# Direct instead of seven-product second matmuls in the first three expert groups of an attention and expert-mixing kernel, with batch 0's chunks in the freed PSUM banks

## The chip, the cores and the metric

The kernel runs on one NeuronCore of one Trainium2 chip, in one launch. The metric is the device time of one execution in microseconds (us). Before the change the median of 9 runs is 932.55 us, with a lowest of 931.42 and a highest of 934.4.

## The reference

Two blocks run one after the other, all in float32. The first is linear attention over batch 4, heads 4, sequence 1088, head size 32, with a feature map that is the outer product of two 8-wide projections. The second is a mixture of 8 experts over the 4352 tokens that the first block leaves, with a Sinkhorn-normalised weight for each token and expert.

```python
phi(x) = outer(S1 x, S2 x)                        # 8 x 8 = 64 features
kv, z  = sum_s phi(k)_s v_s,  sum_s phi(k)_s
attn   = (phi(q) kv) / (phi(q) z + 1e-6)
x      = attn as (4352, 128)
P      = exp(x w_gate - max);  8 rounds of row and column normalisation
out    = sum over e of  P[:, e] * (relu(x w1[e]) w2[e])   # w1: 128x1024, w2: 1024x128
```

## The kernel before

**Where the work is.** Nearly all TensorE work is the two expert products. The first product, `relu(x w1[e])`, is written by `first` (L916), and ScalarE's Relu (L920) moves it from a PSUM bank to the tile `hb` or `hx`. The second product, with `w2[e]`, is written by `into` (L1089). Both are cut into matmuls with 64 output columns. `tile_position` puts each in the left or the right half of the array, so two of them run side by side; I call them half 0 and half 1.

**Fewer products.** A plain block product of the second kind would need eight half matmuls for each block of two hidden slices and two token tiles. `seven` uses a Winograd form with seven. It needs sums and differences of the Relu outputs (`two.sums`, three VectorE instructions a block, L933), sums of the weights (`sums_of_two`, four GpSimd instructions per expert, L203 to L206), and a recombination when a group of tokens is done (`part_of_seven`: seven ScalarE copies at L751 to L766 and six VectorE additions at L742 and L745). `four` and `twenty` do the same with larger blocks in the later part.

**Groups.** `groups` lists token ranges with the experts that are applied to them. The first eight are unweighted: they need no routing weight `P`, so they can run while attention and routing are still going on. Their results go to `kept` and are weighted later. Groups 0 to 2 are 2 x 256 tokens with expert 0, 2 x 288 with expert 0, and 2 x 256 with expert 1, all in batch 0's tokens. Groups 3 to 6 (416 and 384 wide) follow with expert 0, group 7 with expert 1. From `PLAIN` on the groups are weighted and need `P`.

**Order by hand.** The order on VectorE and TensorE is that of the program text (`manual_schedule`). `steps` is a generator that yields after each quarter or eighth of a block. `fill(n)` draws steps from it until their `share` sums to n. Around it the main program lays the steps of the attention: for batch 0 in chunks (`query_products` L382 and L388, `multiply` L397, `fractions` L405, `divide` L416 to L423), and for batches 1 to 3 `keys_ab` (L317, L322), `keys_products` (L334), `keys_sums` (L350), `keys_kept` (L366, L368), `times` (L466), `tops` (L475, L479), `over` (L488 to L494), `transpose_q` (L300), `queries_ab` (L439, L442). Then comes `routing`: the logits (L509), the maximum (L598) and eight rounds (L609 to L625, with TensorE at L619).

**A path through DRAM.** For batches 1 to 3 the projected queries go out to DRAM and come back repeated over partitions: `queries_ab` writes `qa` and `qb` (L446, L450), `repeat_a` reads `ph` (L456) and `repeat_b` reads `rb` (L459). `times` multiplies the two. SyncE's queue (SP) issues most of these transfers, with the loads of `kx`, `qx`, `v` and the weights between them.

**PSUM.** There are eight banks. Four, tag `a`, are shared by everything through `bank()`. Four, tags `s0` to `s3`, hold the sums of a group's second product; `query_products` uses them once for chunk 0.

Of the kernel before, what the change touches and what calls it, by code (L numbers as in the profile page):

```python
# [10 lines left out]
F32 = mybir.dt.float32  # L11
# [39 lines left out]
def kernel(  # L51
# [12 lines left out]
    nc = tc.nc  # L64
# [304 lines left out]

    chunks = ((0, 512), (512, 800), (800, S))  # L370

    def query_products(c, i):


        lo, hi = chunks[c]
        n = hi - lo
        if c == 0:
            banks = [[mps.tile([P, 512], F32, tag=f"s{2 * i + m}", name="s") for m in range(2)] for i in range(2)]
            for m in range(2):
                for i in range(2):  # L380
                    sl = slice(64 * i, 64 * (i + 1))
                    nc.tensor.matmul(banks[i][m][:, 0:n], wqf[sl, m, :], qT[sl, lo:hi], start=True, stop=True,  # L382
                                     tile_position=(64 * i, 0))
        else:
            banks = {i: [bank(), bank()]}
            for m in range(2):
                for s in range(2):
                    nc.tensor.matmul(banks[i][m][64 * s:64 * (s + 1), 0:n],  # L388
                                     wz[:, m, 2 * i + s].rearrange("p i j -> p (i j)"), qT[:, lo:hi],
                                     start=True, stop=True, tile_position=(0, 64 * s))  # L390
        for j in range(2) if c == 0 else (i,):
            nc.scalar.copy(phs[0][:, j, lo:hi], banks[j][0][:, 0:n])
            queries[0, c, j] = banks[j][1][:, 0:n]
# [5 lines left out]
    def fractions(c, m):  # L399

        lo, hi = chunks[c]
        n = hi - lo
        t = queries[0, c, "pn", m] = bank()
        for i in range(2):
            nc.tensor.matmul(t[64 * i:64 * (i + 1), 0:n], kvz[:, m, i].rearrange("p h d -> p (h d)"),  # L405
                             phs[0][:, i, lo:hi], start=True, stop=True, tile_position=(0, 64 * i))
# [177 lines left out]
    def routing():  # L584
# [45 lines left out]
        for b in (1, 0, 2, 3):  # L630
# [15 lines left out]
              *((1088 + 832 * i, 416, 2, [0], False) for i in range(3)), (3584, 384, 2, [0], False),  # L646
              (512, 384, 2, [1], False)]
    PLAIN = len(groups)
    for lo in (1280, 512, 2048, 2816, 3584):
        groups.append((lo, NT3, 3, list(range(2 if lo == 512 else 1, E)), True))  # L650
    groups.append((0, 256, 2, list(range(2, E)), True))
# [3 lines left out]
    items = [(g, e) for g, group in enumerate(groups) for e in group[3]]  # L655
    loaded_w, sources, sums, parts, done = {}, {}, {}, {}, {}
    soon, later = [], []

    def tiles_of(j):
        return groups[items[j][0]][2]  # L660
# [62 lines left out]

    def part(g, k):

        if groups[g][2] == 3:
            part_of_twenty(g, k)
        elif g < len(groups) - 1:
            part_of_seven(g, k)
        else:  # L730
            last_part(g, k)
# [190 lines left out]
    def two(k):  # L922

        j, q = blocks[k]
        n = groups[items[j][0]][1]
        h, ts, (later_h, earlier_h, t13) = hs[k] = room_of(k)

        def step(c):
            f, t = 2 * q + c // 2, c % 2
            first(k, f, t * n, (t + 1) * n, h[c], k % 2)  # L930

        def less(out, a, b):
            nc.vector.tensor_tensor(out, a, b, op=Alu.subtract)  # L933

        def sums(c):

            if k == len(blocks) - 1:
                if c == 4:
                    less(ts[0], h[1], h[0])
                    less(ts[2], h[3], ts[0])  # L940
                    less(ts[1], h[3], h[1])
                    less(ts[3], h[2], ts[2])
            elif c == 4:
                less(t13, later_h, earlier_h)
            elif c == 5:
                less(ts[2], h[3], ts[0])
                less(ts[3], h[2], ts[2])

        return 4, step, sums
# [4 lines left out]
    def four(k):  # L954
        j, q = blocks[k]
        h = hs[k] = room_of(k)
        pqg = hs["pqg"]
        order = ((0, 0), (3, 0), (3, 1), (0, 1), (1, 0), (2, 0), (1, 1), (2, 1))

        def at(f, t):  # L960
            return 4 * t + f

        def step(c):
            f, last = order[c]
            if last:
                first(k, 4 * q + f, 2 * NT3, 3 * NT3, h[:, at(f, 2)], False)
            else:
                first(k, 4 * q + f, 0, 2 * NT3, h[:, f:f + 8:4], False)

        def places(*bs):  # L970
            if len(bs) == 1:
                return h[:, bs[0]]
            if bs[0] == bs[1]:
                return h[:, bs[0]:bs[0] + 1].to_broadcast([P, 2, NT3])
            return h[:, bs[0]:bs[1] + 1:bs[1] - bs[0]]

        def do(out, a, b, off=False):
            nc.vector.tensor_tensor(out if not isinstance(out, tuple) else places(*out), places(*a),  # L978
                                    places(*b) if isinstance(b, tuple) else b, op=Alu.subtract if off else Alu.add)

        def sums(c):
            if c == 2:
                do((U4, U2), (at(0, 0), at(3, 0)), (at(0, 1), at(3, 1)))
            elif c == 3:
                do((U1,), (at(3, 0),), (at(3, 2),))
            elif c == 4:
                do((V4,), (U1,), (at(0, 2),))
            elif c == 6:
                do((V3, V1), (U4, U2), (at(1, 1), at(2, 1)), True)
                do(pqg[:, 0:2], (at(1, 1), at(3, 1)), (at(0, 1), at(2, 1)), True)  # L990
            elif c == 7:
                do((W1, W2), (V4, V4), pqg[:, 0:2])
                do(pqg[:, 2], (V3,), (at(1, 0),), True)
            elif c == 8:
                do((U3, BB), (at(2, 0), at(1, 2)), (at(2, 2), at(2, 2)))
            elif c == 9:
                do((V2, W3), (U3, BB), (at(1, 2), V1))
                nc.vector.tensor_tensor(h[:, W4], pqg[:, 2], h[:, V2], op=Alu.subtract)

        return 8, step, sums  # L1000

    def weighted_of(k):
        return groups[items[blocks[k][0]][0]][4]
# [69 lines left out]
    def into(g, w, x, i, s, place):  # L1073

        lo, n, t, es, _ = groups[g]
        if g not in sums:
            sums[g] = [mps.tile([P, 512], F32, tag=f"s{i}", name="s")[:, 0:n * (t - 1)] for i in range(4)]
            done[g] = {}


        last = g == len(groups) - 1
        seen = done[g]
        c = seen[i, s] = seen.get((i, s), 0) + 1
        per = len(es) * (FO // (4 if t == 3 else 2)) * TIMES[t][i][s]
        if t == 2 and i == 3:
            per //= 2
        if last and (i, s) in ((1, 0), (1, 1), (2, 0), (3, 1)):
            per += 1
        nc.tensor.matmul(sums[g][i][H2 * s:H2 * (s + 1), n * place:n * (place + 1)], w, x, start=c == 1,  # L1089
                         stop=c == per, tile_position=(0, H2 * s))  # L1090
        if c == per:
            seen[i] = seen.get(i, 0) + 1
            if seen[i] == 2:
                part(g, i)
# [4 lines left out]
    def steps():  # L1099

        todo, sums_at, t = {}, {}, 0
        for k in range(len(blocks) + 5):
# [5 lines left out]
            if k < len(blocks):  # L1108
# [3 lines left out]
                if q == 0:  # L1112
                    for i in (j, j + 1, j + 2 if 0 < j and j + 2 < first_weighted else j):
                        if i < len(items) and i not in sources and (pools or i < first_weighted):
                            prepare_x(i)
                        if i < len(items) and i not in loaded_w and (pools or i < first_weighted):
                            prepare_w(i)
                if q == 1 and not weighted and loaded_w.get(j + 1, (0,))[-1] is None:
                    w1, w2, _ = loaded_w[j + 1]
                    loaded_w[j + 1] = w1, w2, sums_of_two(items[j + 1][1], w2)  # L1120
                if q == 0:
                    if weighted and e == es[3 if tiles == 3 else 2]:
                        weigh_kept(g)
                if k == len(blocks) - HELD:
                    kept_to_sums(g)
                m, step, sums_ = (four if tiles == 3 else two)(k)
                products = (twenty if tiles == 3 else seven)
            for c in range(m if k < len(blocks) else 4):
                if k < len(blocks):
                    step(c)  # L1130
# [6 lines left out]
                if k < len(blocks) and c == 0:  # L1137
                    for i in range(2, 10):
                        sums_at.setdefault(t + i, []).append(lambda i=i, f=sums_: f(i))
                    if k < len(blocks) - 2:  # L1140
                        for i, ps in enumerate(products(k)):
                            todo.setdefault(t + LAG + i, []).extend((k, p) for p in ps)
                share = n / 480
                if k >= len(blocks):
                    while later:
                        later.pop(0)()
# [19 lines left out]
    with tc.manual_schedule(engines={engines.DVE, engines.PE, engines.Activation}):  # L1166
# [14 lines left out]
        transpose_q(0, chunks[0][1])  # L1181
        fractions(0, 1)
        queries_ab(1)
        first_w = *first_w[0:2], sums_of_two(0, first_w[1])
        fractions(0, 0)
        query_products(1, 0)
        repeat_a(1)
        repeat_b(1)
        divide(0)
        load_q(2)  # L1190
    with tc.manual_schedule(engines={engines.DVE, engines.PE}):
        fill(0.6)
        multiply(1, 0)
        query_products(1, 1)
        fill(0.6)
        multiply(1, 1)
        transpose_k(1)
        load_k(2)
        fill(0.6)
        fractions(1, 1)  # L1200
        fractions(1, 0)
        keys_ab(1)
        fill(0.6)
        divide(1)
        keys_products(1, 0)
        fill(0.6)
        query_products(2, 0)
        fill(0.6)
        multiply(2, 0)
        query_products(2, 1)  # L1210
        keys_products(1, 1)
        fill(0.6)
        multiply(2, 1)
        fill(0.6)
        fractions(2, 1)
        fractions(2, 0)
        fill(0.6)
        divide(2)
        load_v(2)
        load_q(3)  # L1220
        keys_products(1, 2)
        fill(0.75)
        for b in range(1, B):
            for n in attention(b):
                fill(n)
# [38 lines left out]
```

## Time and profile before

| | before |
|---|---|
| median of 9 runs | 932.55 us (931.42 to 934.4) |
| profiled execution, its own time | 933.92 us |
| its span | 932.1 us |
| mean granted TensorE clock | 0.996 |
| TensorE busy | 919.1 us (99%), 7448 records |
| VectorE busy | 698.0 us (75%) |
| ScalarE busy | 417.5 us (45%) |
| GpSimd busy | 210.5 us (23%) |

A busy line counts the time in which at least one instruction of an engine is under way. Each float32 matmul of the program leaves two records on TensorE, so a pair of matmuls, one in each half, shows as x4. In the profile's names `a` is a tile in the shared banks, `s` one in the sum banks; the arrow points from what is read to what is written. "L916" is a line of the kernel. In a view of waits, "A <- B" means that A stood idle until B was done.

### The profile page before, as it was taken

How to read it: one execution, taken by the hardware profiler on the slowest of the kernel's cores; microseconds unless marked ns; L12 is line 12 of the kernel's file. 1: busy time of each engine (PE TensorE's matmuls, PEld its weight loads, DVE VectorE, ACT ScalarE, POOL GpSimd, SP SyncE). 2: the span in 40 equal slices, each digit the busy share in tenths (PEclk: the TensorE clock that was granted, in tenths of full speed). 3: DMA queues.
4: the chain of work that ended last, by engine and by line, in shares of the span. 5: the costliest groups of instructions: out<-in, count | busy, mean ns of one | idle time of the engine just before them, and what ended most of it. 6: DMA issues, size and time to landing. Idle time of an engine off the chain costs nothing.

```text
span 932.1 us, 18913 instructions
## 1 busy us (share of the span) xinstructions
PE 919.1 (99%) x7448; PEld 576.9 (62%) x7448; DVE 698.0 (75%) x1196; ACT 417.5 (45%) x903; POOL 210.5 (23%) x219
## 2 busy tenths in 40 slices
PE   8989999999999999999999999999999999999997
PEld 6667644567777777765555555555555555556875
DVE  6878689989778888586886656975757977668565
ACT  3345354564444454434544444544445444445443
POOL 4021100056655502130020101201110333210220
PEclk9999999999999999999999999999999999999999
DMA  9886100133345535354353534354434456452640
GB/s 254 262 249 216 53 1 1 30 102 108 108 142 166 181 112 164 108 184 134 120 152 124 176 108 147 111 179 135 137 118 146 151 157 192 158 182 90 173 152 12
DMA packets 91305, 128.15 MB, mean 137 GB/s; under 512 B 25392, under 2 KB 69504, under 8 KB 86480
## 3 DMA queue, kind: packets, MB, share of 16 engines
q1 hardware_dynamic: 88384, 121.42, 41.6%
q0 software_dynamic: 1600, 5.36, 2.0%
q8 instruction: 58, 0.95, 0.4%
q10 hardware_dynamic: 1232, 0.16, 0.1%
q14 instruction: 31, 0.25, 0.1%
HBM read 107.88 MB, written 19.05 MB: 136 GB/s over the span
## 4 chain that ended last, share of the span: by engine, by line
PE 93%; DVE 5%; issue 1%; ACT 1%; POOL 0%; DVEq 0%; ACTq 0%; POOLq 0%
PE a L916 48%; PE s L1089 40%; DVE hb L933 1%; PE a L350 1%; PE a L475 1%; PE a L114 1%; DVE hb L978 1%; PE a L439 0%; PE a L317 0%; ACT hb L920 0%; PE a L509 0%; DVE kp L334 0%; DVE pqg L978 0%; DVE cs L615 0%; PE a L388 0%
## 5 line engine op out<-in xcount | busy, mean ns | idle before, releaser
L916 PE MATMUL a<-xe,w 128*64 128x256 f32 (+1 forms) x2560 | 523.4, 470 | 0.0
L920 ACT ACTIVATE hb<-a 128x256 f32<-128x256 f32 (+4 forms) x408 | 194.8, 479 | 256.9 <-PE a L916 228.8
L920 ACT ACTIVATE hx<-a 128x256 f32<-128x256 f32 (+1 forms) x360 | 167.1, 464 | 214.3 <-PE a L916 195.5
L916 PEld LDWEIGHTS a<-xe,w 128*64 128x64 f32 x2560 | 215.6, 137 | 70.4
L1089 PE MATMUL s<-hb,ws 128*64 128x256 f32 (+3 forms) x1344 | 240.7, 395 | 0.6 <-DVE hb L978 0.6
L1089 PE MATMUL s<-hx,ws 128*64 128x256 f32 x1280 | 207.5, 379 | 0.0
L978 DVE TENSOR_TENSOR hx<-hx 128x512 f32<-128x512 f32 (+1 forms) x204 | 155.0, 770 | 67.7 <-ACT hx L920 62.8
L978 DVE TENSOR_TENSOR hb<-hb 128x512 f32<-128x512 f32 (+1 forms) x204 | 134.9, 672 | 90.7 <-ACT hb L920 86.6
L685 POOL TENSOR_TENSOR xe<-xT,xe 128x768 f32<-128x768 f32 (+2 forms) x41 | 84.9, 2071 | 506.4 <-DMA xe<-pT 385.3
L1089 PEld LDWEIGHTS s<-hb,ws 128*64 128x64 f32 x1344 | 117.3, 137 | 104.7 <-issue 76.5
L1089 PEld LDWEIGHTS s<-hx,ws 128*64 128x64 f32 x1280 | 110.4, 137 | 92.2 <-issue 71.1
L916 PE MATMUL a<-xT,w 128*64 128x416 f32 (+3 forms) x512 | 121.1, 466 | 0.8 <-ACT ab L320 0.6
L1089 PE MATMUL s<-hb,w 128*64 128x256 f32 (+3 forms) x496 | 102.1, 411 | 0.5 <-DVE kept L745 0.5
L933 DVE TENSOR_TENSOR hb<-hb 128x416 f32<-128x416 f32 (+7 forms) x96 | 65.5, 684 | 24.3 <-ACT hb L920 14.6
L1089 PE MATMUL s<-hx,w 128*64 128x256 f32 x384 | 68.9, 379 | 0.0
L916 PEld LDWEIGHTS a<-xT,w 128*64 128x64 f32 x512 | 50.8, 138 | 27.2 <-issue 13.0
L242 POOL TENSOR_TENSOR ws<-w 128x256 f32<-128x256 f32 (+1 forms) x70 | 60.9, 904 | 7.5 <-DMA w<-in_moe_w_dram 4.1
L1089 PEld LDWEIGHTS s<-hb,w 128*64 128x64 f32 x496 | 46.7, 137 | 23.9 <-issue 7.6
L933 DVE TENSOR_TENSOR hx<-hx 128x256 f32<-128x256 f32 (+1 forms) x65 | 38.4, 596 | 25.2 <-ACT hx L920 22.7
L978 DVE TENSOR_TENSOR pqg<-hb 128x512 f32<-128x512 f32 x68 | 45.8, 714 | 0.0
L1089 PEld LDWEIGHTS s<-hx,w 128*64 128x64 f32 x384 | 35.1, 137 | 10.6
L978 DVE TENSOR_TENSOR pqg<-hx 128x512 f32<-128x512 f32 x68 | 36.3, 574 | 0.0
(177 smaller groups left out, 489.9 us busy)
## 6 DMA issues: line engine op xcount, KB each, us to landing
w<-in_moe_w_dram SPq DMA_DIRECT2D x82, 512.0 KB, 5.5
ws<-ws SPq DMA_DIRECT2D x34, 1024.0 KB, 4.9
xe<-pT SPq DMA_DIRECT2D x34, 384.0 KB, 3.9
ws<-ws SPq DMA_DIRECT2D x12, 512.0 KB, 4.6
ph<-qa SPq DMA_DIRECT2D x12, 288.0 KB, 5.8
rb<-qb SPq DMA_DIRECT2D x3, 1152.0 KB, 8.2
pb<-pT SPq DMA_DIRECT2D x6, 384.0 KB, 7.2
kx<-in_k_dram SPq DMA_DIRECT2D x4, 544.0 KB, 4.7
```

Source lines behind the costliest of these rows:

```text
L114: nc.tensor.matmul(warm[:, 0:P], ones, ones, start=True, stop=True)
L242: tc.keep_in_program_order(nc.gpsimd.tensor_tensor(ws[:, c:c + len(ns)], blocks(x), blocks(y), op=Alu.subtract if off else Alu.add))
L350: nc.tensor.matmul(pv[64 * s:64 * (s + 1), i], kp[0:n, H * t + h].rearrange("p i j -> p (i j)"), vx[0:n, slots[h], t, :], start=(t == 0 an ...
L475: nc.tensor.matmul(pn[64 * s:64 * (s + 1), t, 2 * i:2 * i + 2].rearrange("p h d -> p (h d)"), ph[:, i, s, 64 * t:64 * (t + 1)], kvs[b % 2] ...
L685: tc.keep_in_program_order(nc.gpsimd.tensor_tensor(out, x, pb, op=Alu.mult))
L916: nc.tensor.matmul(ph[sl], loaded_w[j][0][:, P * f + H2 * s:P * f + H2 * (s + 1)], sources[j][:, lo:hi], start=True, stop=True, tile_posit ...
L920: nc.scalar.activation(out=out, in_=ph, func=Act.Relu)
L933: nc.vector.tensor_tensor(out, a, b, op=Alu.subtract)
L978: nc.vector.tensor_tensor(out if not isinstance(out, tuple) else places(*out), places(*a), places(*b) if isinstance(b, tuple) else b, op=A ...
L1089: nc.tensor.matmul(sums[g][i][H2 * s:H2 * (s + 1), n * place:n * (place + 1)], w, x, start=c == 1, stop=c == per, tile_position=(0, H2 * s))
```

## The change

The first three groups (`DIRECT`) compute the second product block by block: for each Relu output, two half matmuls with the raw weights, eight per block, accumulated in two banks. Their VectorE sums and recombinations are left out, and `part` copies each finished bank to `kept` on ScalarE. Group 0 uses `s0` and `s1`, group 1 `s2` and `s3`, group 2 `s0` and `s1`. The banks `s2` and `s3` also take batch 0's `query_products(1, 0)` and the `fractions` of chunks 1 and 2. The weight sums of expert 0 are made later, ahead of group 3; those of expert 1 ahead of group 7; expert 1's weights are loaded earlier. The list of steps in which batch 0's chunks 1 and 2 are mixed with `fill` is written anew.

```diff
-    def query_products(c, i):
+    def query_products(c, i, sums=False):
...
-            banks = {i: [bank(), bank()]}
+            banks = {i: [mps.tile([P, 512], F32, tag=f"s{m + 2}", name="s") if sums else bank() for m in range(2)]}
...
-        t = queries[0, c, "pn", m] = bank()
+        t = queries[0, c, "pn", m] = mps.tile([P, 512], F32, tag=f"s{m + 2}", name="s") if c else bank()
...
+    DIRECT = (0, 1, 2)
...
+    def direct_of(j):
+        return items[j][0] in DIRECT
...
     def part(g, k):
-        if groups[g][2] == 3:
+        if g in DIRECT:
+            lo, n, _, es, _ = groups[g]
+            nc.scalar.copy(kept[es[0]][:, lo + k * n:lo + (k + 1) * n], sums[g][k])
+        elif groups[g][2] == 3:
...
         def sums(c):
+            if direct_of(j):
+                return
...
+    def eight(k):
+        j, q = blocks[k]
+        w2, h = loaded_w[j][1], hs[k][0]
+        return [[(w2[:, 2 * q + c // 2, H2 * s:H2 * (s + 1)], h[c], c % 2, s, 0) for s in range(2)] for c in range(4)]
...
-            sums[g] = [mps.tile([P, 512], F32, tag=f"s{i}", name="s")[:, 0:n * (t - 1)] for i in range(4)]
+            banks = range(2 * g, 2 * g + 2) if g in DIRECT else range(4)
+            sums[g] = [mps.tile([P, 512], F32, tag=f"s{i % 4}", name="s")[:, 0:n * (t - 1)] for i in banks]
...
-        if t == 2 and i == 3:
+        if g in DIRECT:
+            per = FO
+        elif t == 2 and i == 3:
...
+                if j == 0 and q == 2:
+                    prepare_w(2)
-                if q == 1 and not weighted and loaded_w.get(j + 1, (0,))[-1] is None:
+                if q == 1 and j + 1 < first_weighted and not direct_of(j + 1) and loaded_w[j + 1][2] is None:
                     w1, w2, _ = loaded_w[j + 1]
-                    loaded_w[j + 1] = w1, w2, sums_of_two(items[j + 1][1], w2)
+                    w = w1, w2, sums_of_two(items[j + 1][1], w2)
+                    loaded_w.update({i: w for i in loaded_w if items[i][1] == items[j + 1][1]})
...
-                products = (twenty if tiles == 3 else seven)
+                products = twenty if tiles == 3 else eight if g in DIRECT else seven
...
-                share = n / 480
+                share = n / 480 * (16 / 15 if g in DIRECT else 1)
...
-        first_w = *first_w[0:2], sums_of_two(0, first_w[1])
         fractions(0, 0)
-        query_products(1, 0)
+        query_products(1, 0, True)
+        query_products(1, 1)
...
-        fill(0.6)
-        multiply(1, 0)
-        query_products(1, 1)
-        fill(0.6)
-        multiply(1, 1)
+        for i in range(2):
+            multiply(1, i)
         transpose_k(1)
         load_k(2)
-        fill(0.6)
+        fill(0.75)
         fractions(1, 1)
         fractions(1, 0)
+        fill(0.75)
+        divide(1)
         keys_ab(1)
-        fill(0.6)
-        divide(1)
+        fill(0.75)
+        query_products(2, 0)
         keys_products(1, 0)
-        fill(0.6)
-        query_products(2, 0)
-        fill(0.6)
+        fill(0.75)
+        query_products(2, 1)
         multiply(2, 0)
-        query_products(2, 1)
         keys_products(1, 1)
-        fill(0.6)
+        fill(0.75)
         multiply(2, 1)
-        fill(0.6)
+        fill(0.75)
         fractions(2, 1)
         fractions(2, 0)
-        fill(0.6)
+        keys_products(1, 2)
+        fill(0.75)
         divide(2)
         load_v(2)
         load_q(3)
-        keys_products(1, 2)
-        fill(0.75)
+        fill(0.5)
```

## The prediction

> **What bounds it.** I read the page first, then windows by stage, TensorE's waits, and timelines of VectorE and SyncE where TensorE waits.
>
> ```profile
> PE 919.1 (99%) x7448; PEld 576.9 (62%) x7448; DVE 698.0 (75%) x1196; ACT 417.5 (45%) x903; POOL 210.5 (23%) x219
> ...
> PE 93%; DVE 5%; issue 1%; ACT 1%; POOL 0%; DVEq 0%; ACTq 0%; POOLq 0%
> ```
>
> TensorE bounds the kernel; only its idle time and its count of matmuls can move the end. The windows (length, then PE, PEld, DVE, ACT, POOL busy, clock, DMA share, GB/s) say where it idles:
>
> ```profile
> 20.00:34.00 14.00, 12.27 (x124) 6.92 (x122) 10.52 (x24) 5.19 (x14) 0.86 (x2) 1.00 0.92 300
> 40.00:55.00 15.00, 15.00 (x196) 12.00 (x192) 13.26 (x25) 8.70 (x23) 5.01 (x8) 1.00 0.87 278
> 55.00:62.00 7.00, 4.51 (x28) 3.29 (x28) 6.54 (x10) 0.82 (x2) 2.21 (x4) 0.76 1.05 346
> 198.00:932.00 734.00, 727.74 (x5652) 456.21 (x5648) 539.08 (x904) 327.25 (x698) 179.90 (x142) 1.00 0.44 139
> ```
>
> Idle time and the only dip of the clock lie before 62 us, and there VectorE is nearly full. TensorE's waits from 20 to 60 us name it:
>
> ```profile
> PE a L439 <- DVE qT L300: 2.5, 1, 2.5
> PE a L405 <- DVE ph L397: 0.9, 2, 0.7
> PE a L916 <- ACT ab L320: 0.6, 1, 0.6
> ```
>
> Here is VectorE's queue ahead of the longest of them (start, length, work):
>
> ```profile
> 52.14 0.43 DVE L745 TENSOR_TENSOR w<-s,r 64x256 f32<-64x256 f32 x1
> 52.60 2.38 DVE L933 TENSOR_TENSOR hb<-hb 128x288 f32<-128x288 f32 x2
> 54.90 0.42 DVE L742 TENSOR_TENSOR z<-z,w 128x256 f32<-128x256 f32 x1
> 55.23 1.22 DVE L334 TENSOR_TENSOR kp<-ab 128x1024 f32<-128x1024 f32 x1
> 56.37 1.30 DVE L300 STREAM_TRANSPOSE qT<-qx 128x1088 f32<-128x1088 f32 x1
> ```
>
> The first three rows are seven-product work, and the change removes them. In the second, one of two instructions took 1.89 us instead of 0.46 while GpSimd made weight sums.
>
> **A ledger of lost time.** I priced every matmul at its steady rate (a pair of half matmuls: 0.43 us at 256 columns, 0.48 at 288, 0.70 at 416, from successive starts in the timeline; 0.11 at 64, from L350's 36 matmuls whose starts span 2.0 us), summed in program order, and subtracted the sum from the trace's start times. Lost time is 3.1 us at batch 1's key projections (start 20.9), 6.7 at its key sums (33.7), 7.1 at its first `tops` (37.9), 10.6 at `queries_ab(3)` (57.8), 13.2 at batch 2's `tops` (70.4), 15.7 at the logits (113.8) and 19.5 at the last routing matmul (180.7). After that it stays between 19.0 and 19.8 to the end. So at most some 16 us can be won, all of it early.
>
> **Part by part: TensorE.** 96 second-product matmuls replace 84. Twelve more half matmuls, eight at 256 and four at 288, are 4 x 0.43 + 2 x 0.48 = 2.7 us, fully on the path.
>
> **VectorE.** Twelve blocks lose three instructions each (0.68 + 2 x 0.42 at 256; 0.76 + 2 x 0.46 at 288, the stretched one aside): 8 x 1.52 + 4 x 1.68 = 18.9 us. Three groups lose six additions of 0.38 to 0.46: 7.5 us. With the stretch this takes 27 to 28 us out of a queue that held TensorE up from 24 to 60 us. ScalarE swaps 21 copies (0.36 to 0.40) for 6 of 0.37 to 0.40; it is busy at most 60% there, so zero.
>
> **GpSimd, SyncE.** Expert 0's four sums (3.0 us) move behind `queries_ab(3)`'s transfers, expert 1's behind `take_over(3)`'s first ones. VectorE, stretched meanwhile, has slack at both places (it idles over 6 us at 112 to 118); if that cover went, one instruction would cost 1.4 us. Expert 1's weights (1 MB) pass ahead of `v` of batch 2 and `qx` of batch 3 on SyncE. They led batch 2's `qa` before as well, so the bytes ahead of that path are the same: zero, up to 2 us if the queue's order hurts.
>
> **Walking the new order.** I follow VectorE and TensorE with the rows' durations. `multiply(1, 1)` (0.45) ends near 18.7, the key transposes (1.24 + 0.20) at 20.1, key projections start at 20.6 (lost: 2.8). `divide(1)` takes 2.0, then products 1.22, multiply 0.45, products 1.22, multiply 0.45, products 0.41, all without block sums between: done at 26.1. TensorE reaches the key sums at 28.5, with 25.6 of work done (27.1 before): lost 2.95 instead of 6.7. They and six pairs of pairs last to about 33.2. Then `tops` needs `times`, and that needs `rb`. A row each of SyncE's timeline (start, length), the page's transfers (KB, us to landing) and VectorE's timeline:
>
> ```profile
> 25.62 0.40 SPq L459 DMA_DIRECT2D rb<-qb  x1
> ...
> rb<-qb SPq DMA_DIRECT2D x3, 1152.0 KB, 8.2
> ...
> 33.92 0.94 DVE L466 TENSOR_TENSOR ph<-ph,rb 128x768 f32<-128x768 f32 x1
> ```
>
> 25.6 + 8.2 = 33.8: `rb` lands just as VectorE was ready before. Nothing ahead of it in SyncE's queue changes, so this wait takes the place of the ones removed: `times` 33.9 to 34.8, the copy of `kvs` to 35.1, `tops` at 35.2 with 30.15 of work done. Lost: 5.1, with 2.0 us of stall. From there VectorE is ahead: `queries_ab(2)` finds its transpose done at 37.3, its matmuls come at 38.6, batch 2's keys near 48.0. Its `ab` copy ends at 50.0, product 1.22, transpose 1.30: `queries_ab(3)` at 52.5, where TensorE comes at 51.9. A wait of 0.6 instead of 2.5; lost 6.2.
>
> For batch 2's `tops` (62.3) `rb` must be there by 61. Before, it was issued at 52.04, so about 60.2; I take it as in time. Between `tops` and logits 2.5 us were lost before, in steps of 0.25 to 0.4 mostly where a lone seventh half matmul meets an attention step beginning on the same half. With eight there is no lone half until group 3; I keep 1.5 (bounds 0.5 and 2.5). Logits and routing cost 3.8 before; VectorE is 90% busy there as before, so I keep 3.4 (bounds 2.5 and 5). Lost at the last routing matmul: 6.3 + 1.5 + 3.4 = 11.2 instead of 19.5. The weights' chain from there (14.1 us to the weighted `xe` before) meets 20.4 us of work instead of 16.9.
>
> **The clock.** The stall of 2.49 us was followed by 3.4 us at a clock of 0.5, which lost 1.6 us. The new 2.0 us stall lies between that and the 0.7 us one at 30, which had no such effect: 0 or 1.6. I take 0, as the idle time is spread on both sides of a boundary of the 3.4 us steps in which the clock's record changes, and keep 1.6 for the range.
>
> The Trainium skill, "TensorE: Matmul & The Clock Gate", section "What's actually happening", has the clock halve after an idle window of about 3.4 us. By that rule neither stall would halve it; the trace shows it after 2.49 us, so the row decides, and by the rule alone the 1.6 us would drop from the range.
>
> **Sum.** Lost time 11.2 - 19.4 = -8.2 (19.4 being the level at which it stays), work +2.7: -5.5 us. The profiled execution took 933.92, so 928.4 beside it; it lies 1.4 above the median of 932.55, so 927.0 for the median.
>
> **Rivals.** *The front wait only moves.* `rb` of batch 2 is 2 us late as well and the clock halves once: -5.5 + 2 + 1.6 = -1.9, 930.6, and with routing at its bound of 5, 932. For it: DMA is full from 20 to 62 us. Against: after the first `tops` the transfers start 2 to 3 us earlier than before.
>
> *Same-half neighbours, slower.* `eight` always issues half 0 then 1, while `first` flips in odd blocks; the new order has 40 more places in the direct groups where two successive matmuls use the same half. If each cost half a pair, 0.22 to 0.24, that is 9 us: +3.5, 936. It decides from 5.5 / 40 = 0.14 us each. Against it, the end of the weighted groups has eight such places from 846.9 to 850.3:
>
> ```profile
> 846.89 0.60 PE L916 MATMUL a<-xe,w 128*64 128x256 f32 x4
> 847.32 0.60 PE L1089 MATMUL s<-hb,ws 128*64 128x256 f32 x4
> 847.75 0.60 PE L916 MATMUL a<-xe,w 128*64 128x256 f32 x4
> 848.18 0.60 PE L1089 MATMUL s<-hb,ws 128*64 128x256 f32 x4
> ```
>
> Starts stay 0.43 apart, so I price it at zero.
>
> *More is won.* If the steps between `tops` and logits vanish (1.0 less) and logits and routing fall to their bound of 2.5 (0.9), with the 0.6 wait gone too: -8, 924.5.
>
> *It doesn't do what it says.* The freed banks may serve nothing: before, no wait longer than 0.6 us was for a shared bank. Then all of the gain is VectorE's, and the time is the forecast's.
>
> **Numbers.** Forecast (925 to 929.5) 0.70; front wait moves 0.15; same-half or another slower mechanism 0.09; more is won 0.06. The range 923.5 to 932.0 holds the first, the second and most of the last. A measurement here tells 0.2%, 1.9 us, from no change: faster means under 930.7, slower over 934.4. Half of the second case lies under 930.7: 0.70 + 0.06 + 0.07 = 0.83; the rest of it and a few mixed cases 0.09; slower 0.08.
>
> **What would show it.** Right: no wait of `queries_ab(3)` over 1 us; batch 1's key sums near 28.5, its first `tops` near 35 behind `rb`; a half clock at most once; weighted work from about 192 instead of 197.5. Wrong: TensorE pairs further apart than 0.43 in odd direct blocks, `tops` of batch 2 waiting for `rb`, or more than 5 us lost in logits and routing.

## The result, and the profile after

After the change the median of 10 runs is 928.36 us (927.69 to 929.28). Beside it the kernel before had a median of 933.3 over 31 runs (931.26 to 934.8). The ratio is 0.9951, 95% interval 0.9943 to 0.9959: faster by 0.5%, well outside the 0.2% that a measurement can tell. The forecast was 927.0 with a range of 923.5 to 932.0.

The profiled execution took 927.69 us, with a span of 925.8 and a mean clock of 0.999. It is the lowest of the ten. The page, busy times and the shares of the chain:

```profile
PE 914.8 (99%) x7472; PEld 557.6 (60%) x7472; DVE 673.6 (73%) x1142; ACT 412.6 (45%) x888; POOL 212.3 (23%) x219
...
PE 95%; DVE 3%; issue 1%; ACT 1%; POOL 0%; ACTq 0%; DVEq 0%; POOLq 0%
```

VectorE lost 24.4 us (27 to 28 predicted) and 54 instructions. Not all of what was left out shows, since the block sums of the later groups (L989, L978 before) took 5.2 us more in sum than before. TensorE has 24 records more, the 12 half matmuls, and the chain runs through VectorE for 3% instead of 5%. The same stretches as in the prediction (length, then PE, PEld, DVE, ACT, POOL busy, clock, DMA share, GB/s):

```profile
20.00:34.00 14.00, 13.41 (x196) 10.12 (x192) 8.25 (x19) 6.16 (x17) 0.00 (x0) 1.00 0.94 328
40.00:55.00 15.00, 14.69 (x178) 11.73 (x176) 6.36 (x9) 6.47 (x17) 2.36 (x5) 1.00 0.99 324
55.00:62.00 7.00, 6.86 (x114) 4.80 (x112) 2.83 (x4) 2.33 (x8) 1.30 (x3) 1.00 1.00 230
90.00:125.00 35.00, 33.90 (x248) 15.50 (x245) 25.58 (x48) 16.22 (x33) 6.35 (x9) 1.00 0.12 35
198.00:925.00 727.00, 721.72 (x5612) 432.12 (x5608) 532.96 (x897) 324.45 (x692) 171.82 (x134) 1.00 0.44 140
```

VectorE was busy 13.3 of 15 us from 40 to 55; now it is 6.4. From 55 to 62 TensorE is busy 6.86 us instead of 4.51, and the clock does not dip. The fourth row is new: from 90 to 125 us TensorE now idles 1.1 us, with VectorE at 25.6 of the 35 us. Before, it had no idle time there at all:

```profile
90.00:125.00 35.00, 35.00 (x336) 19.96 (x334) 22.91 (x42) 15.91 (x35) 4.77 (x9) 1.00 0.19 52
```

TensorE's waits after the change, over the whole span (us in total, times, longest), name it:

```profile
PE s L1109 <- DVE kept L754: 1.7, 3, 1.1
PE a L475 <- ACT hb L929: 1.1, 2, 0.6
...
PE a L439 <- DVE qT L300: 0.3, 1, 0.3
```

The wait of `queries_ab(3)` (L439) fell from 2.5 to 0.3 us. On top now is `kept` (L754): the recombination of a seven-product group, for which the next group's first sums wait. VectorE's queue around the two `times` that open batches 1 and 2:

```profile
32.72 0.96 DVE L466 TENSOR_TENSOR ph<-ph,rb 128x768 f32<-128x768 f32 x1 [4.44 <-DMA rb<-qb]
...
59.10 0.96 DVE L466 TENSOR_TENSOR ph<-ph,rb 128x768 f32<-128x768 f32 x1 [6.79 <-DMA v<-in_v_dram]
```

VectorE stood idle for 4.4 and 6.8 us ahead of them. The second row names a `v` transfer, but L466 reads only `ph` and `rb`; the transfer it needs is that of `rb`, issued at 48.66.

Priced as in the prediction's ledger, work is 908.3 us instead of 905.6, and the lost time goes as follows.

| place | predicted start, lost | measured start, lost |
|---|---|---|
| batch 1's key projections | 20.6, 2.8 | 20.1, 2.4 |
| batch 1's key sums | 28.5, 2.95 | 28.2, 2.7 |
| batch 1's first `tops` | 35.2, 5.1 | 34.0, 3.9 |
| `queries_ab(3)` | 52.5, 6.2 | 51.0, 4.7 |
| batch 2's first `tops` | 62.3, 6.3 | 61.7, 5.7 |
| logits | lost 7.8 | 105.2, 7.1 |
| last routing matmul | lost 11.2 | 170.5, 10.1 |
| last matmul | lost 11.2 | lost 11.4 |

Before, lost time at the last matmul was 20.4. So the profiled pair differs by -9.0 + 2.7 = -6.3 us, which is the difference of the spans (932.1 and 925.8). Of the 9.0 us, 1.6 are the half clock that this one execution of before held.

### The profile page after: what moved, and what is told of

Read it like the earlier page. It is cut to its first block, busy times and chain, and to the rows that moved or that the text cites. A ratio compares the mean times of both kernels' runs of the same rounds, so it can differ in the third digit from the quotient of the medians.

```text
span 925.8 us, 18890 instructions
## 1 busy us (share of the span) xinstructions
PE 914.8 (99%) x7472; PEld 557.6 (60%) x7472; DVE 673.6 (73%) x1142; ACT 412.6 (45%) x888; POOL 212.3 (23%) x219
## 4 chain that ended last, share of the span: by engine, by line
PE 95%; DVE 3%; issue 1%; ACT 1%; POOL 0%; ACTq 0%; DVEq 0%; POOLq 0%
PE a L925 49%; PE s L1109 41%; PE a L350 1%; PE a L475 1%; PE a L114 1%; DVE hb L942 1%; DVE hb L989 1%; PE a L317 0%; PE a L439 0%; PE a L388 0%; PE s L405 0%; ACT hb L929 0%; DVE pqg L989 0%; DVE cs L615 0%; PE a L509 0%
## 5 line engine op out<-in xcount | busy, mean ns | idle before, releaser
L925 PE MATMUL a<-xe,w 128*64 128x256 f32 (+1 forms) x2560 | 518.1, 470 | 0.0
L925 PEld LDWEIGHTS a<-xe,w 128*64 128x64 f32 x2560 | 207.7, 137 | 79.4 <-issue 0.2
L1109 PE MATMUL s<-hb,ws 128*64 128x256 f32 (+2 forms) x1248 | 215.5, 395 | 0.2 <-DVE hb L989 0.2
L989 DVE TENSOR_TENSOR hx<-hx 128x512 f32<-128x512 f32 (+1 forms) x204 | 158.6, 788 | 64.5 <-ACT hx L929 59.3
L989 DVE TENSOR_TENSOR hb<-hb 128x512 f32<-128x512 f32 (+1 forms) x204 | 133.7, 666 | 95.0 <-ACT hb L929 90.8
L1109 PEld LDWEIGHTS s<-hx,ws 128*64 128x64 f32 x1280 | 106.0, 137 | 98.8 <-issue 73.3
L1109 PEld LDWEIGHTS s<-hb,ws 128*64 128x64 f32 x1248 | 102.5, 137 | 102.7 <-issue 77.3
L1109 PE MATMUL s<-hb,w 128*64 128x256 f32 (+3 forms) x616 | 116.0, 406 | 1.7 <-DVE kept L754 1.7
L925 PE MATMUL a<-xT,w 128*64 128x416 f32 (+3 forms) x512 | 117.2, 462 | 0.1
L1109 PEld LDWEIGHTS s<-hb,w 128*64 128x64 f32 x616 | 54.1, 137 | 30.0 <-issue 9.7
L242 POOL TENSOR_TENSOR ws<-w 128x256 f32<-128x256 f32 (+1 forms) x70 | 60.2, 896 | 15.3 <-PE a L925 10.6
L925 PEld LDWEIGHTS a<-xT,w 128*64 128x64 f32 x512 | 48.7, 137 | 24.4 <-issue 15.3
L942 DVE TENSOR_TENSOR hb<-hb 128x416 f32<-128x416 f32 (+3 forms) x60 | 47.3, 789 | 14.5 <-ACT hb L929 11.8
L942 DVE TENSOR_TENSOR hx<-hx 128x256 f32<-128x256 f32 (+1 forms) x65 | 38.7, 600 | 24.8 <-ACT hx L929 23.7
L989 DVE TENSOR_TENSOR pqg<-hb 128x512 f32<-128x512 f32 x68 | 47.5, 739 | 0.0
L989 DVE TENSOR_TENSOR pqg<-hx 128x512 f32<-128x512 f32 x68 | 37.4, 590 | 0.0
```

The costliest lines, as they stand in the source:

```text
L242: tc.keep_in_program_order(nc.gpsimd.tensor_tensor(ws[:, c:c + len(ns)], blocks(x), blocks(y), op=Alu.subtract if off else Alu.add))
L925: nc.tensor.matmul(ph[sl], loaded_w[j][0][:, P * f + H2 * s:P * f + H2 * (s + 1)], sources[j][:, lo:hi], start=True, stop=True, tile_posit ...
```

## The experiments

Each was timed beside the kernel before on the same chip. The sets of experiments ran on four chips, so kernels of different sets are compared by their ratios first. Lost time is that of each kernel's own profiled execution, at five places, and so of one execution: for no_block_sums, two_direct and alternate_halves it took 1.2 to 1.4 us less than their medians, for four_direct 3.8 more.

| kernel | ratio to before, 95% | work | key sums 1 | `tops` 2 | logits | last routing | end |
|---|---|---|---|---|---|---|---|
| before | 1 | 905.6 | 6.7 | 13.2 | 15.7 | 19.5 | 20.4 |
| the change | 0.9951 (0.9943 to 0.9959) | 908.3 | 2.7 | 5.7 | 7.1 | 10.1 | 11.4 |
| direct_only | 0.9953 (0.9939 to 0.9967) | 908.3 | 3.3 | 6.2 | 6.8 | 10.3 | 11.6 |
| order_only | 0.9969 (0.9959 to 0.9979) | 905.6 | 5.3 | 9.8 | 12.6 | 15.9 | 16.5 |
| no_block_sums | 0.9974 (0.9963 to 0.9986) | 905.6 | 3.0 | 7.6 | 9.9 | 13.9 | 14.3 |
| shared_banks | 0.9960 (0.9946 to 0.9975) | 908.3 | 3.1 | 7.3 | 8.7 | 11.7 | 12.4 |
| one_direct | 0.9953 (0.9941 to 0.9964) | 906.4 | 3.1 | 7.2 | 9.6 | 14.5 | 15.1 |
| two_direct | 0.9961 (0.9949 to 0.9973) | 907.4 | 2.4 | 5.3 | 6.5 | 10.6 | 12.4 |
| alternate_halves | 0.9953 (0.9940 to 0.9966) | 908.3 | 2.5 | 5.6 | 7.1 | 10.1 | 10.8 |
| no_rb_1_late | 0.9935 (0.9922 to 0.9948) | 908.3 | 2.8 | 4.8 | 6.2 | 9.2 | 10.6 |
| four_direct | 0.9936 (0.9921 to 0.9950) | 909.7 | 2.8 | 8.5 | 10.8 | 10.9 | 12.6 |
| five_direct | 0.9954 (0.9940 to 0.9967) | 911.0 | 2.9 | 7.7 | 8.4 | 8.2 | 8.9 |
| four_direct_old_order | 0.9932 (0.9919 to 0.9944) | 909.7 | 3.5 | 6.3 | 7.0 | 8.3 | 9.3 |

**Which part of the change gains: direct_only, order_only, no_block_sums, shared_banks.** *direct_only* is before with the direct products of groups 0 to 2 alone:

```diff
+    DIRECT = (0, 1, 2)
...
-        first_w = *first_w[0:2], sums_of_two(0, first_w[1])
```

> The direct products of the first three groups alone: the hand-written order of batch 0's chunks and the shared banks are those of before. My theory (the gain is VectorE's queue, emptied of 27 us of sums): nearly all of the gain stays, 928.5 to 930.5 us, key sums of batch 1 start by 29.5 us and no wait of queries_ab(3) over 1 us. Rival (freed banks and the new order bring the gain): at best half of it, 931 us or more.

Measured: 928.04 us (927.44 to 929.09), below what was expected, and the same as the change. The key sums came at 29.7, a little behind the 29.5 that was named. The direct products alone, with what they leave out on VectorE and the later weight sums on GpSimd, carry the whole gain. Their waits:

```profile
PE s L1109 <- DVE kept L754: 3.3, 4, 1.7
...
PE a L475 <- DVE kvs L366: 0.9, 1, 0.9
...
PE a L439 <- DVE qT L300: 0.2, 1, 0.2
```

*order_only* is the change without direct products: the new order of batch 0's steps, its sum banks and the early load of expert 1's weights remain, with expert 0's sums early as before.

```diff
-    DIRECT = (0, 1, 2)
+    DIRECT = ()
...
+        first_w = *first_w[0:2], sums_of_two(0, first_w[1])
```

> The new order and the sum banks for batch 0's chunks alone: all groups keep seven products, with the weight sums of expert 0 made early as before. VectorE theory: the queue is as full as before, 931.5 to 935 us, and TensorE waits again for VectorE between 24 and 60 us. Rival (order and banks bring the gain): 925 to 928 us, since the 2.7 us of extra products are saved too.

Measured: 929.94 us (929.3 to 930.22). Both sides missed: the order without any direct product gains 0.3% by itself. Its waits:

```profile
PE s L1109 <- DVE kept L754: 2.4, 3, 1.2
PE a L439 <- DVE qT L300: 1.5, 1, 1.5
PE a L317 <- DVE kT L305: 1.4, 1, 1.4
```

The key sums come 2 us earlier than before, the wait of `queries_ab(3)` is 1.5 instead of 2.5, and there was no dip of the clock. But the two parts do not add. In lost time the order alone saves 3.9 us, the direct products alone 8.7, both together 9.0, each with the 1.6 us of before's half clock in it. They remove largely the same waits.

*no_block_sums* is before with the block sums of groups 0 to 2 left out, so that the seven products read the Relu outputs instead; the recombinations stay.

```diff
         def sums(c):
+            if items[j][0] < 3:
+                return
...
         h, ts, _ = hs[k]
+        if items[j][0] < 3:
+            ts = h
```

> The kernel before, but the first three groups leave out the sums of Relu outputs on VectorE and feed the Relu outputs themselves to the seven products, so part of the computation is left out; product count, order and banks are those of before. VectorE theory: 19 of the 27 us leave the queue and no product is added, so 925.5 to 928 us, lost time at the end of routing 12 to 14 us instead of 19.5. Rival (banks and order): over 930 us.

Measured: 929.82 us (928.56 to 932.02), later than expected. The lost time at the last routing matmul, 13.9, is inside the 12 to 14 that was named. The key sums come at 30.0 instead of 33.7, so the block sums account for the front. By the medians they are worth 2.6 us, where direct_only gains 4.4 with 2.7 of added products; so they are only part of what the direct products save. The recombinations, and VectorE work beside GpSimd's weight sums, remain in this kernel, and so does this wait:

```profile
PE a L439 <- DVE qT L300: 1.5, 1, 1.5
```

Its timeline shows what keeps it. One addition of a recombination, two instructions ahead of the transpose (L300), took 2.11 us instead of 0.42, while GpSimd made expert 1's weight sums (48.2 to 50.3 us):

```profile
48.49 2.11 DVE L742 TENSOR_TENSOR z<-z,w 128x256 f32<-128x256 f32 x1
50.53 1.21 DVE L334 TENSOR_TENSOR kp<-ab 128x1024 f32<-128x1024 f32 x1
```

That is 1.7 us, as much as the whole wait. In order_only the product at L334 took 2.81 us instead of 1.22 at the same place, also beside those sums, and in before an L933 instruction 1.89 instead of 0.46. In the change expert 1's sums run at 100 us or later, so part of what it gains at `queries_ab(3)` may be their move; the move alone was not tried.

*shared_banks* is the change with batch 0's chunks in the shared banks again:

```diff
-        t = queries[0, c, "pn", m] = mps.tile([P, 512], F32, tag=f"s{m + 2}", name="s") if c else bank()
+        t = queries[0, c, "pn", m] = bank()
...
-        query_products(1, 0, True)
+        query_products(1, 0)
```

> The changed kernel with batch 0's chunks back in the four shared banks, order as changed. VectorE theory: 0 to 1.5 us slower than the changed kernel, 928.4 to 930 us. Rival (the freed banks matter): the gain falls by half or more, 931 us or more, with new waits of TensorE for a shared bank between 18 and 28 us.

Measured: 928.68 us (928.23 to 930.18). The interval covers the change's ratio: what the freed banks serve is worth 0.3 us by the medians and 0.8 by the ratios, not told from nothing.

**How many groups: one_direct and two_direct.** Only `DIRECT` differs.

```diff
-    DIRECT = (0, 1, 2)
+    DIRECT = (0,)
```

> The changed kernel with only group 0 direct. 1.8 us of extra products go; 9.4 us of group 1's sums return to VectorE between 40 and 62 us, where it is busy 9 of 22 us. VectorE theory: key sums of batch 1 still near 28.5 us and 926.8 to 928.6 us, with at most 1 us more wait at queries_ab(3). Rival (what counts is the number of sums, in proportion): the mean between the order alone and the whole change, 929.4 us.

> The changed kernel with only groups 0 and 1 direct; group 2 keeps seven products. 0.9 us of extra products go; about 8.6 us of sums return to VectorE between 62 and 90 us, where it is busy 13 of 28 us. VectorE theory (sums cost nothing where the queue has room): 927.3 to 928.6 us. Rival (any sum in the attention's stage delays TensorE): 929 us or more.

Measured: 928.82 us (927.63 to 929.41) with group 0 alone, 929.49 (928.31 to 930.03) with groups 0 and 1. Both lie above the theory's ranges, and the second where its rival had it; the kernel before was at 933.51 beside them. By the ratios one group does as well as three. With two, 0.9 us less work than with three met 1.0 us more lost time, most of it here:

```profile
PE s L1109 <- DVE kept L754: 3.9, 4, 1.7
```

That is the first hint at the later experiments: what the front gains is partly lost again at the ends of seven-product groups.

**Neighbours on one half: alternate_halves.** `eight` issues the halves in the order of `first`, so that the two never meet on the same half.

```diff
-... for s in range(2)] for c in range(4)]
+... for s in ((1, 0) if k % 2 else (0, 1))] for c in range(4)]
```

> The changed kernel with the two half matmuls of a direct product issued in the order that the first products of the same block use, so that no two successive matmuls of a direct block use the same half. My pricing (such neighbours cost nothing): within 0.5 us of the changed kernel. Rival of the prediction (0.22 us each, 40 of them): 919 to 920 us.

Measured: 928.42 us (927.07 to 930.56). From the start of batch 1's key sums to the last routing matmul it took 142.4 us, the change 142.2. The rival of 9 us is out: these neighbours cost nothing.

**The wait for `rb`: no_rb_1 and no_rb_1_late.** In *no_rb_1* GpSimd fills `rb` with ones for batch 1 instead of the transfer; batch 1's query products are left out of the computation.

```diff
+    nc.gpsimd.memset(rb, 1.0)
...
     def repeat_b(b):
+        if b == 1:
+            queries.pop(b)
+            return
```

> The changed kernel without the transfer of rb for batch 1: GpSimd fills the tile with ones, so batch 1's query products are left out of the computation. Theory (the DMA chain to rb took the place of the removed waits): the first tops no longer waits (0.8 to 1.2 us), later transfers move up by up to 4 us so that batch 2's tops loses its wait of about 1 us too: 926 to 927.5 us. Rival (TensorE would wait there for something else): 928 us or more.

Measured: 927.88 us (927.45 to 928.76), ratio 0.9945 (0.9933 to 0.9957), between the two. The step at the first `tops` had gone (lost 4.0 to 4.4, instead of 2.7 to 3.9), but the key sums were already 1.3 us late. The fill itself did that, at the very start. GpSimd's row, and then VectorE's rows in the same kernel:

```profile
2.18 2.02 POOL L134 MEMSET rb<- 128x2304 f32 x1
```

```profile
3.18 1.82 DVE L34 TENSOR_SCALAR mant<-raw 128x64 uint32<-128x64 uint32 x1 [1.43 <-DMA raw<-in_S_dram]
3.29 1.74 DVE L35 TENSOR_SCALAR expo<-raw 128x64 uint32<-128x64 uint32 x1
```

The two instructions take 0.20 and 0.19 us in the change. The Trainium skill, "SBUF — State Buffer", section "Who interferes with whom", says that such `tensor_scalar` forms can use a port pair that VectorE shares with GpSimd and that the later of the two is blocked outright; the rows agree that VectorE was held up, by 1.6 us. The fill ended at 4.2 and VectorE's two instructions at 5.0, with GpSimd's short fills, which the long one had moved back, between them. So the experiment took away one wait and added another. *no_rb_1_late* leaves the transfer out in the same way, but lets VectorE fill `rb`, in the idle time ahead of `times`:

```diff
     def times(b, c):
+        if b == 1 and c == 0:
+            nc.vector.memset(rb, 1.0)
```

> Batch 1's rb is not read back; VectorE fills the tile with ones just before the first multiplication with it, in the 4.4 us in which it stands idle for rb in the changed kernel (batch 1's query products are therefore left out of the computation). Nothing is added at the kernel's start this time, where the GpSimd fill stretched two VectorE instructions from 0.20 to 1.8 us and cost 1.1 us. Theory (the wait for rb costs the changed kernel the step of 1.2 us in lost time from 2.7 to 3.9 us at batch 1's first tops, and that much stays): lost time at the first tops 2.7 to 3.2, at the end 10 to 10.7, median 0.6 to 1.2 us below the changed kernel's, 927.0 to 927.8. Rival (whatever the front gains is given back at later waits): lost time at the end within 0.4 of the changed kernel's 11.35, median 928.0 to 928.7.

Measured: 926.94 us (926.64 to 927.28), 1.4 below the change's median (the intervals of the two ratios just overlap), with lost time of 3.2 at the first `tops`:

```profile
28.83 1.98 DVE L470 MEMSET rb<- 128x2304 f32 x1 [0.43 <-issue]
30.85 0.96 DVE L471 TENSOR_TENSOR ph<-ph,rb 128x768 f32<-128x768 f32 x1
```

In the change the transfer of batch 1's `rb` is the new end of the front's waits, as the prediction had it. Most of what the front would gain without it stays to the end.

**The ends of the groups: four_direct, five_direct, four_direct_old_order.** The lost time of the change rises by 3.0 us between the logits and the last routing matmul, in steps of 1.3 at 118.5, 0.6 at 140.4 and 0.7 at 162.0. The first of them on VectorE and on TensorE, one timeline each:

```profile
115.17 2.28 DVE L942 TENSOR_TENSOR hb<-hb 128x832 f32<-128x832 f32 x3
117.37 0.58 DVE L754 TENSOR_TENSOR z<-s,z 128x416 f32<-128x416 f32 x1
117.87 0.57 DVE L754 TENSOR_TENSOR kept<-s,m 64x416 f32<-64x416 f32 x1
```

```profile
118.50 0.56 PE L1109 MATMUL s<-hb,w 128*64 128x416 f32 x1 [1.10 <-DVE kept L754]
```

Routing's reductions and the block sums of group 4 stand ahead of group 3's recombination, and group 4's first sum needs the bank that the recombination still reads. A direct group has no recombination. *four_direct* makes group 3 direct as well:

```diff
-    DIRECT = (0, 1, 2)
+    DIRECT = (0, 1, 2, 3)
```

> Group 3 is direct as well (416 columns, banks s2 and s3). Work: four more half matmuls at 416, 4 x 0.35 = 1.4 us. VectorE loses 4 blocks of block sums and six additions there, some 12 us. Theory (the three steps of lost time in the routing stage, 1.3 us at 118.5, 0.6 at 140.4 and 0.7 at 162.0 in the changed kernel, are the ends of groups 3, 4 and 5, where the next group's first sums wait for a bank that VectorE's recombination still reads; a direct group has no recombination): the wait at 118.5 is gone, lost time at the last routing matmul 8.3 to 9.0 instead of 10.1, the end at work +1.4 and lost -1.1 to -1.8: 928.0 to 928.8, no difference that can be told from the changed kernel. Rival (that lost time comes from the logits and the routing itself, on whichever group they fall): lost time stays near 10, median 929.4 to 930.2.

Measured: 926.5 us (925.86 to 930.29), better than expected, and by the median better than the change. The intervals of the two ratios overlap (to 0.9950 and from 0.9943); five of the six times lie below all ten of the change. From the logits (10.8) to the last routing matmul (10.9) the lost time no longer rises, and TensorE idles no more there:

```profile
62.00:70.00 8.00, 6.29 (x84) 4.80 (x82) 4.51 (x8) 1.75 (x5) 1.59 (x3) 0.79 0.98 231
...
90.00:125.00 35.00, 35.00 (x298) 16.24 (x296) 14.60 (x31) 13.64 (x28) 5.76 (x9) 1.00 0.13 35
```

The last row shows VectorE at 14.6 us instead of 25.6. The first row needs a word: this profiled execution, 930.29, is the slowest of its six, the others being at 925.86 to 926.79. In it batch 2's `rb` was late:

```profile
63.22 0.96 DVE L466 TENSOR_TENSOR ph<-ph,rb 128x768 f32<-128x768 f32 x1 [9.74 <-DMA rb<-qb]
```

`tops` then lost 2.6 us, and a half clock after it 1.7 more. That is the prediction's second case, both halves of it, in one execution.

*five_direct* has group 4 in `DIRECT` too, and *four_direct_old_order* is direct_only with group 3.

> Groups 0 to 4 are direct: 1.4 us more work than with four, and some 12 us less on VectorE at the end of group 4. With four direct groups the lost time did not rise at all between the logits and the last routing matmul (10.83 and 10.87 us in its profiled execution). Theory (only those waits could be won): nothing is left for the fifth group to win there, its work is paid in full, 927.5 to 928.2. Rival (VectorE's load in the routing stage still delays what follows, the two steps of 0.8 us in the weighted part): those steps shrink, 926 to 927, no slower than four_direct.

> direct_only with group 3 direct as well: before's order of batch 0's steps, its shared banks, no early load of expert 1's weights. Theory (what the change gains is VectorE's unloading; order and banks add nothing to it, and group 3 adds the routing stage's waits): the same step as from the change to four_direct, 926 to 927 us, no wait of a sum bank for a recombination near 118 us. Rival (the new order or the early load is what lets group 3 pay): 927.8 to 929.

Measured: 927.87 us (927.5 to 928.98) with five, 1.4 above the median of four_direct, as expected when the fifth group's 1.4 us of work is paid in full. The intervals of these two ratios overlap as well. With four groups in before's order: 926.04 us (925.41 to 926.93), the lowest of all the kernels. New order, sum banks and early load add nothing to the direct products. In before's order VectorE had batch 2's `rb` before TensorE came to `tops`. The first row is four_direct_old_order's, the second direct_only's:

```profile
57.75 0.96 DVE L466 TENSOR_TENSOR ph<-ph,rb 128x768 f32<-128x768 f32 x1 [3.29 <-DMA rb<-qb]
```

```profile
57.03 0.96 DVE L466 TENSOR_TENSOR ph<-ph,rb 128x768 f32<-128x768 f32 x1 [2.71 <-DMA rb<-qb]
```

There `rb` of batch 2, issued at 49.7 and 49.5, was used 8.0 and 7.5 us later, ahead of need. In the change, shared_banks, alternate_halves, four_direct and five_direct it was issued at 48.7 to 52.1 and used 10.2 to 12.2 us later. In these five, 1 MB of weights passes near 27 instead of 50. But two_direct, with the same load at 26.3 and the same order of transfers, issued `rb` at 48.2 and used it 7.7 us later, and no_rb_1_late used it 8.1 us after issue. So neither the early load nor the order of transfers is shown to delay it, and what does stays open. TensorE waited for it only in the profiled executions of four_direct and five_direct, 1.7 us each. In the other three the first product and the copy of `kvs` were done 0.1 to 1.4 us before TensorE came to `tops`.

## Why the prediction was right, step by step

**VectorE's load at the front.** Right. The key sums came at 28.2 (28.5 predicted), `queries_ab(3)` waited 0.3 us (0.6), and direct_only shows that the direct products, without the new order and the banks, carry the gain. How it divides between the block sums, the recombinations and the stretch beside GpSimd's weight sums is shown only in part (no_block_sums).

**`rb` takes the place of the waits removed.** Right, and shown by no_rb_1_late. Its size was off: the page's median of 8.2 us was taken, and it landed after 7.2, which put the first `tops` at 34.0 instead of 35.2.

```profile
rb<-qb SPq DMA_DIRECT2D x3, 1152.0 KB, 7.2
```

**`rb` of batch 2 "as in time".** Right for the change. It was issued 3.4 us earlier than before and VectorE waited 6.8 us for it, but the product was done at 60.1, the copy of `kvs` at 60.3, and TensorE came to `tops` at 61.7. The step in lost time was 0.95 us all the same, where the sum had about 0.1. About half of it is two places just ahead of `tops`, where TensorE's pairs start 0.74 and 0.72 us apart instead of 0.48, each time as a Relu ends (60.47 and 61.66). The same gaps stand in two_direct, which used its `rb` at 55.9, so they aren't `rb`'s. They are absent in direct_only, with before's order.

**Between `tops` and logits, 1.5.** Right in sum, 1.4, but not in kind. There were no steps for lone half matmuls; 1.1 of it is one step at batch 3's `tops`.

**Logits and routing, 3.4.** Measured 3.0, but not as before. The bank waits at the ends of seven-product groups are 1.7 us of it by the view of waits, where before had one of 0.5 in its 3.8, and the steps at these waits add up to 2.6. With group 3 direct the term is gone (four_direct). The prediction kept it as it was and so missed that one more direct group pays for itself.

**Lost time after routing.** Taken as constant, at 19.4; it rose by 1.2 us (before by 0.9, to 20.4 at the last matmul). Weighted work began at 190.7, not near 192.

**The clock.** Right for the change: no dip. But the half clock of 1.6 us in the profiled execution of before was counted as if every execution had it. In the four sets of runs of before beside the experiments, 6 of 18, 5 of 11, none of 11 and 1 of 9 show a mean clock of 0.996, as that execution did. In the first two sets these have medians of 933.7 and 933.9, the others, at 0.998 or more, 931.9 and 932.9; the set with none has 932.8. So about a quarter of the executions have it, at 1 to 1.8 us by the first two sets, and of the change's ten none falls below 0.998. Of the 1.6 us the median could gain perhaps a quarter; that is an estimate from these counts.

**The sum.** The profiled pair differs by 6.2 us in its own time, against 5.5 predicted. Medians differ by 4.9 us against the 31 runs. The two are apart because before's profiled execution, the one with the half clock, lay 0.6 above its median of 31, and the change's, the lowest of its ten, 0.7 below its own. The 31 runs also put before 0.75 above the 932.55 of the prediction; against that number, 928.36 is 1.4 above 927.0. Part of the agreement along the way is luck: lost time at the first `tops` was put 1.2 us too high, the step at batch 2's 0.85 too low.

**What the change says and what it does.** The rival "it doesn't do what it says" was half right. The freed banks are worth little or nothing (shared_banks), and the gain is that of the direct products. What no rival foresaw is that the new order alone, with seven products, would also gain 0.3%.

**Left open.** Why the two later bank waits (140.4 and 162.0 in the change) vanish with group 3 direct too, though groups 4 and 5 keep their recombinations, was not tried. four_direct_old_order still loses 1.3 us over the same stretch, with a wait of 0.3 us for block sums (L942) in it and none for a recombination. Nor was why two_direct is no better than one_direct: the intervals overlap.

## What to carry to other kernels

Saving products on the bounding engine can cost more than it saves where the sums around them hold up that engine's next work; count the waits, not only the products, and choose group by group. Here, by the medians, the first four groups are better direct and a fifth is not. Where one profiled execution carries an accident, such as a half clock, subtract only the share of the runs that have it.

## What was not expected of the hardware

A stall of 1.7 us shown in the waits was followed by a half clock in one execution of four_direct and by none in one of five_direct, at the same place. The clock's record changes in steps of 3.41 us, and the share of a step seems to matter. In the step just ahead of the half clock TensorE was busy 0.92 us in before (54.8 to 58.2) and 1.61 us in four_direct (61.3 to 64.7). In the steps that hold the next longest stalls it was busy 1.69 us in two_direct (115.2 to 118.6), 1.72 in direct_only (115.4 to 118.8) and 1.76 in five_direct (61.6 to 65.0), and the clock stayed full. A limit near half a step fits all five; with so few cases, and with ends of matmuls that the profile models, it is not shown. A GpSimd fill held up two VectorE instructions of 0.2 us for 1.6 us each, although they touch other data. GpSimd's weight sums stretched single VectorE instructions by 1.4 to 1.7 us in before, order_only and no_block_sums, each time just ahead of TensorE's longest wait for VectorE's transpose.
